# An edge mask written by VectorE into the scores' bank in place of a mask product on TensorE

## The chip, the cores and the metric

The kernel runs on one core of a Trainium2 chip. The metric is the device time of one launch in microseconds (us). Before the change it is 702.63 us, the median of three runs (699.69 to 703.38).

A core has a matrix engine (TensorE, PE in the profile; its weight loads have a row of their own, PEld), VectorE (DVE), ScalarE (ACT), GpSimd (POOL) and SyncE (SP), which issues the DMAs. Each takes its instructions in the order of the program, and semaphores between them hold an instruction until its inputs are there.

## The reference

One transformer block with modulation by a condition vector (2048 rows, width 448, 16 heads of 28, feed-forward width 1792). The part that the change touches is attention within a window:

```
scores = einsum("bhqd,bhkd->bhqk", q, k) * (Dh ** -0.5)
mask = (idx[:, None] - idx[None, :] >= 0) & (idx[:, None] - idx[None, :] < W)     # W = 256
scores = where(mask, scores, -1e9)
p = softmax(scores, axis=-1)
o = einsum("bhqk,bhkd->bhqd", p, v)
```

A query attends to itself and to the 255 rows before it. Around it stand a layer norm with scale and shift, the products with wqkv and wo, a second layer norm and a feed-forward network with Mish.

## The kernel before

All large products run as several passes over values split into a high and a low half. The 2048 rows are worked on in four groups of 512 (g = 0 to 3). The qkv products of a group are written to DRAM with keys and queries transposed, and loaded per head.

Attention walks over 64 slots (16 heads of each of 4 groups; a slot is called a head below), and each head over three units b = 0, 1, 2, so that u = 3 x head + b. A unit is one bank of 512 columns of scores, keys along the partitions and queries along the columns. BLOCKS says which 128-row key blocks against which 128-row query tiles share the bank: the outer units hold a block three tiles wide and one a single tile wide, the middle unit two blocks two tiles wide. In group 0 the blocks before the first row are missing, so the middle unit holds one block, in columns 256 to 511.

B(u), line 733, makes a unit. It takes one of two banks (tag sB, in turn), multiplies keys and queries into it (L742; the first product overwrites the bank, the next ones add), and then adds the mask: an identity matrix (identr) is the stationary operand and a strip of fdmask the moving one, so that the product puts 0 or -2^100 onto the scores. fdmask has two triangles, one for the far edge of the window (key too old) and one for the diagonal (key too new), 128 columns each. In groups 1 to 3 the outer units get by with one product over two separate strips of 128 columns (L753), since some rows of the operands carry a part of their mask; the middle unit has its far triangle in columns 128 to 255 and its diagonal in 256 to 383, and one product of 256 columns covers both (L757). In group 0 the middle unit has the diagonal alone, one product of 128 columns on the same line, and the outer units have theirs there too. ScalarE then takes the exponential of the bank twice, to P in f32 and to Ph, the high half (L760 and L761).

The order on the engines is written out by hand. In the step of unit u the program issues, in this order: what is due of earlier small work (pipe.step: splits of the qkv products, layer norm outputs); the products of the low parts with the values for unit u - 3 (PV, L778) and, at a head's end, the copy-out of its sums (EV, L784); B(u); the subtraction P - Ph for unit u - 1 on GpSimd (SP, L768); the first scores of a head three ahead (A, L711, in one of two banks with tag sA), whose row maxima VectorE takes under a mask (L713, tile mx); at some heads the transposition of these maxima (M2, L719); a share of the filler work (the qkv products of the next group, the products with wo of the group before, L315, and transpositions, L250), by a credit of so much per unit; a piece of side work (layer norms, L241 and L220, weight sums, L175); and the products of the high parts for unit u - 2.

VectorE's queue in this stretch therefore holds, in the order of issue: low halves of the fillers (L339, L369, L262, L647), the reductions (L713), the small splits of the maxima (L721, L722), the sums for the outputs (L805, L806) and the side work.

The mask fdmask is made once at the start: fdf is a piece of a weight buffer (wmf) that is free by then; GpSimd clears it (L463) and cuts the two triangles (L464, L466), and ScalarE copies it twice, side by side, into the 512 columns of fdmask in bf16 (L513).

Of the kernel before, what the change touches and what calls it, by code (L numbers as in the profile page):

```python
# [11 lines left out]
AF = mybir.ActivationFunctionType  # L12
ALU = mybir.AluOpType
# [38 lines left out]
def adaln_block(ctx: ExitStack, tc: tile.TileContext, x, wqkv, wo, w1, b1, w2, c, w_mod, out):  # L52
    nc = tc.nc
    PE, ACT, DVE, POOL = nc.tensor, nc.scalar, nc.vector, nc.gpsimd
# [37 lines left out]
    def bank(tag, bufs, name):  # L92
        return PS[0].tile([128, 512], F32, name=name, tag=tag, bufs=bufs)
# [18 lines left out]
    for k in range(4):  # L112
        wmf = st0.tile([128, 2 * D], F32, name=f"wm01_{k}")
# [11 lines left out]
    two = wqkv[:, 128:1152].rearrange("r (a n) -> r a n", n=512)[:, :, 0:256]  # L125
# [30 lines left out]
    identr = kq.tile([128, 128], BF16, name="identr")  # L156
    fdmask = kq.tile([128, 512], BF16, name="fdmask")
# [301 lines left out]
    for v in V:  # L459
        POOL.memset(v[:, :, 28:29].bitcast(F32), 1.0)  # L460
        POOL.memset(v[:, :, 29:32].bitcast(F32), 0.0)
    fdf = wmf[:, 0:256]
    POOL.memset(fdf[:, 0:256], 0.0)  # L463
    POOL.affine_select(fdf[:, 128:256], fdf[:, 128:256], pattern=[[-1, 128]], compare_op=ALU.is_ge, fill=-2.0 ** 100,  # L464
                       base=-1, channel_multiplier=1)
    POOL.affine_select(fdf[:, 0:128], fdf[:, 0:128], pattern=[[1, 128]], compare_op=ALU.is_ge,  # L466
                       fill=-2.0 ** 100, base=0, channel_multiplier=-1)


# [40 lines left out]
    flush()  # L510
    split_cols(*QCOLS[2], (POOL, POOL, DVE, DVE))
    for c in (0, 256):
        ACT.activation(fdmask[:, c:c + 256], fdf, AF.Copy)  # L513
    st0_s.close()
    att, att_s = pool("att")
    Q2 += [att.tile([128, 2, GT], F32R, name=f"q2_{i}") for i in range(1, NQ // 2)]
# [26 lines left out]
    def two(v, c, step):  # L543
        return bass.AP(v.tensor, v.offset + c, [list(v.ap[0]), [step, 2], [1, 128]])
# [182 lines left out]
    def units(g, b):  # L727
        return [x for x in BLOCKS[b] if g > 0 or x[0] >= 2]

    def by_width(blocks):  # L730
        return sorted(blocks, key=lambda x: x[2] - x[1])

    def B(u):
        i, b = divmod(u, 3)
        g, h = divmod(i, H)
        q, k = Q3[i % NQ], K3[i % NK]
        bl = units(g, b)
        c0 = bl[0][3]
        rows = 86 if g == 0 else 128
        p = bank("sB", 2, f"sB{u}")  # L740
        for n, (jj, t0, t1, c) in enumerate(by_width(bl)[::-1]):
            PE.matmul(p[:, c:c + 128 * (t1 - t0)], k[0:rows, jj * 128:(jj + 1) * 128], q[0:rows, t0 * 128:t1 * 128],  # L742
                      start=(n == 0), stop=False, skip_group_check=True)
        far = {c + 128 * (jj - t0) for jj, t0, t1, c in bl if t0 <= jj < t1}
        diag = {c + 128 * (jj - 2 - t0) for jj, t0, t1, c in bl if t0 <= jj - 2 < t1}
        masked = []
        for c in sorted(far | diag):
            if c in far:
                masked.append((256 if c + 128 in diag else 128, c, 128))
            elif c - 128 not in far:  # L750
                masked.append((128, c, 0))
        if g and b != 1:
            PE.matmul(two(p, (64, 0)[b // 2], 320), identr, two(fdmask, (192, 0)[b // 2], 192), start=False, stop=True,  # L753
                      skip_group_check=True)
            masked = []
        for n, c, m in sorted(masked):
            PE.matmul(p[:, c:c + n], identr, fdmask[:, m:m + n], start=False, stop=True, skip_group_check=True)  # L757
        P = Pt[u] = att.tile([128, 512], F32, name=f"P{u}", tag="P", bufs=3)
        Ph[u] = att.tile([128, 512], F32R, name=f"Ph{u}", tag="Ph", bufs=3)
        ACT.activation(P[:, c0:], p[:, c0:], AF.Exp, scale=SCALE)  # L760
        ACT.activation(Ph[u][:, c0:], p[:, c0:], AF.Exp, scale=SCALE)  # L761
# [7 lines left out]

    def PV(u, P):  # L770
        i, b = divmod(u, 3)
        g, h = divmod(i, H)
        if P is Ph and b == 0:
            pvb[i] = bank("sA", 2, f"pv{i}") if NS - 3 <= i < NS - 1 else bank("pv", 1, f"pv{i}")
        pv = pvb[i]
        for n, (jj, t0, t1, c) in enumerate(by_width(units(g, b))):
            j = 4 * g - 2 + jj
            PE.matmul(pv[0:60, t0 * 128:t1 * 128], V[j % NV][:, h, :], P[u][:, c:c + 128 * (t1 - t0)],  # L778
                      start=(P is Ph and b == 0 and n == 0), stop=False, skip_group_check=True)

# [287 lines left out]
    for u in range(NU + 9):  # L1068
        s, k = divmod(u, 3)
        g = s // H  # L1070
# [8 lines left out]
        if u < NU:  # L1079
            B(u)  # L1080
# [28 lines left out]
        if to_copy and u % 6 == 5:  # L1109
            t, p = to_copy.pop(0)  # L1110
# [20 lines left out]
    p1 = FW["p1"]  # L1131
# [65 lines left out]
    for n in range(NN + 1):  # L1197
        g, f = divmod(n, NF)
# [47 lines left out]
```

## Time and profile before

| what | value |
|---|---|
| timed runs | 699.69, 702.63, 703.38 us |
| profiled execution, its own time | 699.71 us |
| its span in the trace | 698.0 us |
| attention stretch | about 48 to 403 us |
| score products of B (L742) | 352, 73.7 us busy |
| mask products (L753 and L757) | 96 and 128 |
| row-maximum reductions (L713) | 256, mean 527 ns |
| exponentials (L760 and L761) | 192 each, means 571 and 568 ns |
| low parts on GpSimd (L768) | 192, mean 1232 ns |

A row of a group gives line, engine, operation, output and inputs by the program's names, shapes, count, then busy time and the mean duration of one, and last the idle time of the engine before them with what ended it. A row of the timeline gives start, duration, engine, line, operation and, in brackets, an idle time ahead and its releaser. Durations of products on TensorE are whole flights through a pipelined array: products follow each other at shorter distances than these.

### The profile page before, as it was taken

Reading aid. Unit: us, or ns where it says so; the run is one execution under the profiler, and the core shown is the slowest. Engines: PE = TensorE matmul, PEld = TensorE weight load, DVE = VectorE, ACT = ScalarE, POOL = GpSimd, SP = SyncE. Lnnn points to the kernel's source line nnn. Section 1 sums busy time; section 2 is a strip of 40 time slices with the busy share of each in tenths; the row PEclk is TensorE's granted clock in tenths of the full one; section 3 lists DMA queues with packets and bytes.
Section 4 is the critical chain, followed back from the end, with each engine's and each line's share of the span. In section 5 each row is a group of like instructions: output and inputs, shape, how many; then the busy total and the mean of one; then the engine's idle time right before and its main releaser. Section 6 shows DMA issues by size and latency. Waiting matters only on the chain.

```text
span 698.0 us, 11835 instructions
## 1 busy us (share of the span) xinstructions
PE 679.1 (97%) x3905; PEld 583.6 (84%) x3905; DVE 382.2 (55%) x1030; ACT 391.7 (56%) x741; POOL 334.0 (48%) x372
## 2 busy tenths in 40 slices
PE   8899999999999999999999899999999999999997
PEld 8777788888888888888887688888888888888886
DVE  5688657688665887655768754553125212521112
ACT  4638788777667867667878874353224222422221
POOL 7846779686766776666779967222010000000000
PEclk9999999999999999999999999999999999999999
DMA  7865665365662462763773165810250035001001
GB/s 213 263 226 198 217 213 176 119 201 164 179 206 85 156 211 89 191 211 108 226 217 112 53 211 173 212 29 4 103 120 1 2 105 121 0 2 53 0 1 53
DMA packets 75568, 91.13 MB, mean 131 GB/s; under 512 B 31632, under 2 KB 51838, under 8 KB 75508
## 3 DMA queue, kind: packets, MB, share of 16 engines
q1 hardware_dynamic: 75044, 90.38, 42.5%
q8 instruction: 31, 0.51, 0.3%
q14 instruction: 29, 0.24, 0.1%
q10 hardware_dynamic: 464, 0.00, 0.0%
HBM read 56.60 MB, written 32.51 MB: 128 GB/s over the span
## 4 chain that ended last, share of the span: by engine, by line
PE 82%; DVE 6%; DMA 4%; issue 2%; ACT 2%; POOL 1%; SPq 1%; POOLq 0%; DVEq 0%; ACTq 0%
PE z L950 21%; PE pv L778 9%; PE qk L315 7%; PE acc L1142 7%; PE acc L1140 6%; PE acc L1141 6%; PE sA L711 5%; PE wo L315 5%; PE sB L742 4%; PE qk_v L315 4%; DMA scr<-st 2%; DVE junk L713 2%; PE et L792 2%; PE warm L428 1%; PE sB L753 1%
## 5 line engine op out<-in xcount | busy, mean ns | idle before, releaser
L768 POOL TENSOR_TENSOR Pl<-P,Ph 128x512 fp32r<-128x512 f32 (+2 forms) x192 | 235.0, 1232 | 77.5 <-ACT Ph L761 44.9
L713 DVE CUSTOM_DVE_ANT_0 junk<-sA,mask 128x384 f32<-128x384 f32 (+2 forms) x256 | 135.0, 527 | 91.9 <-PE sA L711 84.5
L760 ACT ACTIVATE P<-sB 128x512 f32<-128x512 f32 (+2 forms) x192 | 109.6, 571 | 58.8 <-PE sB L757 33.7
L958 DVE TENSOR_TENSOR al<-t,ah 128x512 fp32r<-128x512 f32 x56 | 39.2, 699 | 188.6 <-ACT ah L957 188.6
L956 ACT ACTIVATE t<-z,b1c 128x512 f32<-128x512 f32 x56 | 38.4, 686 | 142.9 <-PE z L950 142.6
L761 ACT ACTIVATE Ph<-sB 128x512 fp32r<-128x512 f32 (+2 forms) x192 | 109.0, 568 | 0.0
L711 PE MATMUL sA<-k,q 84*128 84x384 f32 (+2 forms) x256 | 100.7, 396 | 2.6 <-DVE mx L713 1.8
L950 PE MATMUL z<-hlf,w 128*128 128x512 f32 x224 | 88.5, 395 | 0.0
L950 PE MATMUL z<-hhf,w 128*128 128x512 f32 x224 | 88.5, 395 | 0.0
L1140 PE MATMUL acc<-w2h,ah 128*128 128x448 f32 x224 | 82.0, 366 | 0.0
L1142 PE MATMUL acc<-w2h,al 128*128 128x448 f32 x224 | 81.9, 366 | 0.0
L1141 PE MATMUL acc<-w2l,ah 128*128 128x448 f32 x224 | 81.5, 364 | 0.0
L778 PE MATMUL pv<-Ph,v 128*60 128x256 f32 (+2 forms) x352 | 76.7, 292 | 0.6 <-ACT o L784 0.3
L778 PE MATMUL pv<-Pl,v 128*60 128x256 f32 (+2 forms) x352 | 73.8, 283 | 2.9 <-POOL Pl L768 2.0
L742 PE MATMUL sB<-q,k 128*128 128x256 f32 (+1 forms) x352 | 73.7, 283 | 0.6 <-DMA q<-mr 0.6
L950 PE MATMUL z<-hhf,w1l 128*128 128x512 f32 x168 | 66.3, 394 | 0.0
L742 PEld LDWEIGHTS sB<-q,k 128*128 128x128 f32 (+1 forms) x352 | 61.2, 188 | 2.0 <-DMA q<-mr 1.0
L778 PEld LDWEIGHTS pv<-Ph,v 128*60 128x60 f32 x352 | 45.7, 133 | 14.1 <-ACT o L784 1.9
L711 PEld LDWEIGHTS sA<-k,q 84*128 84x128 f32 x256 | 49.6, 195 | 8.0 <-DVE mx L713 5.3
L778 PEld LDWEIGHTS pv<-Pl,v 128*60 128x60 f32 x352 | 45.1, 132 | 11.9 <-POOL Pl L768 4.0
L950 PEld LDWEIGHTS z<-hlf,w 128*128 128x128 f32 x224 | 42.1, 188 | 10.1
L224 POOL COPY xn<-xn 128x64 f32<-128x64 f32 x12 | 4.5, 396 | 93.7 <-DVE xn L241 93.6
(167 smaller groups left out, 1305.0 us busy)
## 6 DMA issues: line engine op xcount, KB each, us to landing
scr<-st SPq DMA_DIRECT2D x24, 512.0 KB
k<-scr SPq DMA_DIRECT2D x48, 252.0 KB
q<-scr SPq DMA_DIRECT2D x64, 168.0 KB
scr<-st SPq DMA_DIRECT2D x32, 256.0 KB
x<-x1d SPq DMA_DIRECT2D x10, 448.0 KB
xin<-in_A_x_dram SPq DMA_DIRECT2D x8, 448.0 KB
xr<-in_A_x_dram SPq DMA_DIRECT2D x16, 224.0 KB
x1d<-xr SPq DMA_DIRECT2D x16, 224.0 KB
```

The lines of the kernel that those rows point to most:

```text
L315: PE.matmul(p, b, a, start=(n == 0), stop=(n == 10))
L711: PE.matmul(p[:, c0:384], q[0:84, t * 128:(t + 1) * 128], k[0:84, t * 128 + c0:t * 128 + 384], start=True, stop=True)
L713: DVE.tensor_tensor_reduce(out=junk[:, c0:384], in0=p[:, c0:384], in1=mask[:, c0:384], scale=1.0, scalar=-3.0e38, op0=ALU.add, op1=ALU.max ...
L742: PE.matmul(p[:, c:c + 128 * (t1 - t0)], k[0:rows, jj * 128:(jj + 1) * 128], q[0:rows, t0 * 128:t1 * 128], start=(n == 0), stop=False, ski ...
L760: ACT.activation(P[:, c0:], p[:, c0:], AF.Exp, scale=SCALE)
L761: ACT.activation(Ph[u][:, c0:], p[:, c0:], AF.Exp, scale=SCALE)
L768: eng.tensor_tensor(Pl[u][:, a:b], Pt[u][:, a:b], Ph[u][:, a:b].bitcast(F32), op=ALU.subtract)
L778: PE.matmul(pv[0:60, t0 * 128:t1 * 128], V[j % NV][:, h, :], P[u][:, c:c + 128 * (t1 - t0)], start=(P is Ph and b == 0 and n == 0), stop=F ...
L950: PE.matmul(zb[n], ps[m][1], ps[m][0], start=(m == 0), stop=(m == 10))
L1140: PE.matmul(p, ah[n][:, ts], w2h[f], start=(f == 0), stop=False)
L1141: PE.matmul(p, ah[n][:, ts], w2l[f], start=False, stop=False)
L1142: PE.matmul(p, al[n][:, ts], w2h[f], start=False, stop=(f == NF - 1))
```

## The change

In the step of a head's first unit (b = 0, except for the very first head), behind that unit's products, the bank of the next unit, the middle one, is taken at once, and VectorE copies the mask into it, over all its columns: 512 in groups 1 to 3, 256 in group 0. When the middle unit's turn comes, its first product no longer overwrites the bank but adds to it, and its mask product is left out. For this the mask is laid out as the middle unit needs it: 128 columns of zero, the far triangle, the diagonal, 128 columns of zero. The outer units' products keep their form and read their strips at other places of it. The middle unit of the first head keeps its mask product.

```diff
-    fdf = wmf[:, 0:256]
-    POOL.memset(fdf[:, 0:256], 0.0)
+    fdf = wmf[:, 0:512]
+    POOL.memset(fdf, 0.0)
     POOL.affine_select(fdf[:, 128:256], fdf[:, 128:256], pattern=[[-1, 128]], compare_op=ALU.is_ge, fill=-2.0 ** 100,
                        base=-1, channel_multiplier=1)
-    POOL.affine_select(fdf[:, 0:128], fdf[:, 0:128], pattern=[[1, 128]], compare_op=ALU.is_ge,
+    POOL.affine_select(fdf[:, 256:384], fdf[:, 256:384], pattern=[[1, 128]], compare_op=ALU.is_ge,
                        fill=-2.0 ** 100, base=0, channel_multiplier=-1)
...
     for c in (0, 256):
-        ACT.activation(fdmask[:, c:c + 256], fdf, AF.Copy)
+        ACT.activation(fdmask[:, c:c + 256], fdf[:, c:c + 256], AF.Copy)
...
+    seeds = {}
+
     def B(u):
...
-        p = bank("sB", 2, f"sB{u}")
+        seeded = u in seeds
+        p = seeds.pop(u) if seeded else bank("sB", 2, f"sB{u}")
         for n, (jj, t0, t1, c) in enumerate(by_width(bl)[::-1]):
             PE.matmul(p[:, c:c + 128 * (t1 - t0)], k[0:rows, jj * 128:(jj + 1) * 128], q[0:rows, t0 * 128:t1 * 128],
-                      start=(n == 0), stop=False, skip_group_check=True)
+                      start=(n == 0 and not seeded), stop=False, skip_group_check=True)
...
-                masked.append((128, c, 0))
-        if g and b != 1:
-            PE.matmul(two(p, (64, 0)[b // 2], 320), identr, two(fdmask, (192, 0)[b // 2], 192), start=False, stop=True,
-                      skip_group_check=True)
+                masked.append((128, c, 256))
+        if g and b != 1 and not seeded:
+            c, d, m, n = ((64, 320, 192, -64), (320, -320, 192, 64))[b // 2]
+            PE.matmul(two(p, c, d), identr, two(fdmask, m, n), start=False, stop=True, skip_group_check=True)
             masked = []
-        for n, c, m in sorted(masked):
+        for n, c, m in sorted(masked) if not seeded else ():
             PE.matmul(p[:, c:c + n], identr, fdmask[:, m:m + n], start=False, stop=True, skip_group_check=True)
+        if u and b == 0:
+            p1 = seeds[u + 1] = bank("sB", 2, f"sB{u + 1}")
+            d = units(g, b + 1)[0][3]
+            DVE.tensor_copy(p1[:, d:], fdmask[:, d:])
```

## The prediction

> **What bounds the kernel now.** I read the page's head and its chain of work first, then the busy time of the attention stretch, where every edit of the change lies.
>
> ```profile
> PE 679.1 (97%) x3905; PEld 583.6 (84%) x3905; DVE 382.2 (55%) x1030; ACT 391.7 (56%) x741; POOL 334.0 (48%) x372
> ...
> PE 82%; DVE 6%; DMA 4%; issue 2%; ACT 2%; POOL 1%; SPq 1%; POOLq 0%; DVEq 0%; ACTq 0%
> ```
>
> TensorE (PE) is busy 97% of the span and holds 82% of the chain that ended last; VectorE (DVE) holds only 6% of it. A product that is taken away from PE should therefore shorten the kernel by nearly its own time, as long as nothing else makes PE stand still. But the mean hides the stage: VectorE's work is crowded into the attention stretch, from 48 to 403 us.
>
> ```profile
> 48.00:403.00 355.00, 344.10 (x2308) 294.22 (x2307) 255.62 (x787) 271.28 (x549) 261.71 (x246) 1.00 0.54 167
> ```
>
> The columns after the length are PE, weight loads (PEld), DVE, ACT and POOL. PE is at 97% with a granted clock of 1.00, and DVE is at 255.62 of 355, that is 72%. So the change takes work from the engine at 97% and gives work to one at 72%, in a stretch where PE already waits for DVE at a few places:
>
> ```profile
> PEld sA L711 <- DVE mx L713: 5.3, 13, 0.8
> ...
> PEld pv L778 <- POOL Pl L768: 4.0, 7, 0.8
> ...
> PEld mt L719 <- DVE mx L713: 2.4, 3, 0.9
> ...
> PEld pv L778 <- ACT o L784: 1.9, 5, 0.6
> ```
>
> The columns are microseconds in total, times, and the longest. PE's waits on the row-maximum reductions (mx) come to 5.3 + 2.4 = 7.7 us; those on POOL and ACT, which this change doesn't touch, to 5.9 us.
>
> **What is removed.** The middle unit of each head (b = 1) loses its mask product and the load of the identity for it, except in head 0. The first row below holds this form's 64 wide products: 48 of them are middle units of groups 1 to 3; the other 16 lie in the last units of group 0 and stay. Of the 64 narrow ones 15 go.
>
> ```profile
> L757 PE MATMUL sB<-fdmask,identr 128*128 128x256 bf16 x64 | 18.0, 281 | 0.0
> L757 PE MATMUL sB<-fdmask,identr 128*128 128x128 bf16 x64 | 12.0, 228 | 0.0
> ```
>
> The 281 ns are a pipelined product's whole flight, not its price. The price is what it adds to the distance between its neighbours' starts, which the timeline shows:
>
> ```profile
> 247.64 0.28 PE L757 MATMUL sB<-fdmask,identr 128*128 128x256 bf16 x1
> ...
> 247.64 0.20 PEld L711 LDWEIGHTS sA<-k,q 84*128 84x128 f32 x1
> 247.68 0.42 PE L711 MATMUL sA<-k,q 84*128 84x384 f32 x1
> ...
> 247.94 0.37 PE L315 MATMUL wo<-wo,hlo 128*128 128x448 f32 x1
> ...
> 248.56 0.34 PE L711 MATMUL sA<-k,q 84*128 84x384 f32 x1
> ...
> 248.73 0.40 PE L778 MATMUL pv<-Ph,v 128*60 128x128 f32 x2
> ```
>
> From the mask product to the product behind the sA product there are 247.94 - 247.64 = 0.30 us; an sA product without a mask ahead takes 248.73 - 248.56 = 0.17 to its follower. The rows have two digits, so 0.13 is good to 0.02; I take 0.12. For the narrow form, of half the columns, I take 0.07, an estimate between a half of that and the whole. The sum: 48 x 0.12 + 15 x 0.07 = 5.8 + 1.0 = 6.8 us off PE, all in the stretch where PE is at 97%. The bounds are 48 x 0.11 + 15 x 0.06 = 6.2 and 48 x 0.13 + 15 x 0.12 = 8.0.
>
> **What is added.** 63 writes of VectorE from bf16 in SBUF to f32 in PSUM: 512 columns in 48 heads, 256 in 15. The trace has no such form. The nearest rows:
>
> ```profile
> L254 DVE TENSOR_SCALAR tr<-tr,cols 128x512 f32<-128x512 f32 x14 | 11.4, 812 | 0.7 <-ACT hh L257 0.7
> ...
> L713 DVE CUSTOM_DVE_ANT_0 junk<-sA,mask 128x256 f32<-128x256 f32 x16 | 6.7, 417 | 3.0 <-PE sA L711 2.7
> ...
> L254 DVE TENSOR_SCALAR zt<-zt,cols 128x512 f32<-128x512 f32 x12 | 6.3, 523 | 0.0
> ...
> L786 DVE COPY o<-pv 60x512 f32<-60x512 f32 x3 | 2.1, 684 | 0.1
> ```
>
> The plain copy of 512 columns with one side in PSUM took 684 ns. The same tensor_scalar (L254) took 523 ns with both sides in SBUF and 812 with both in PSUM; these two are my ends. I take 0.68 and, from the 256-column row, 0.42: 48 x 0.68 + 15 x 0.42 = 32.6 + 6.3 = 38.9 us more on DVE, which takes it from 72% to (255.6 + 38.9) / 355 = 83% of the stretch.
>
> [...]
>
> Most of these microseconds are hidden under PE. What counts is whether a write is done when PE comes to the middle unit's score products. The write goes to the bank that the last unit of the head before has used, so it starts when two things are over: ACT's second exponential of that unit (Ph, L761), and whatever stands ahead of it in DVE's in-order queue. It must be done before the first sB product (L742) of the middle unit. With 0.05 us after the release and 0.06 from its end to PE, I worked this through for all 63 heads on the trace's own times. Four of them, each as the release by ACT, where it matters the DVE instruction ahead, and the middle unit's first product:
>
> ```profile
> 55.14 0.59 ACT L761 ACTIVATE Ph<-sB 128x512 fp32r<-128x512 f32 x1
> ...
> 56.46 0.69 DVE L262 TENSOR_TENSOR hl<-tr,hh 128x512 fp32r<-128x512 f32 x1
> 56.48 0.28 PE L742 MATMUL sB<-q,k 86*128 86x256 f32 x1
> ```
>
> ```profile
> 250.51 0.59 ACT L761 ACTIVATE Ph<-sB 128x512 fp32r<-128x512 f32 x1
> ...
> 251.33 1.44 DVE L241 TENSOR_SCALAR xin<-xin,mva,rsa 128x448 f32<-128x448 f32 x1
> ...
> 252.96 0.40 PE L742 MATMUL sB<-q,k 128*128 128x256 f32 x2
> ```
>
> ```profile
> 330.64 0.59 ACT L761 ACTIVATE Ph<-sB 128x512 fp32r<-128x512 f32 x1
> ...
> 331.28 0.68 DVE L339 TENSOR_TENSOR st<-qk,st 128x512 fp32r<-128x512 f32 x1
> ...
> 332.86 0.40 PE L742 MATMUL sB<-q,k 128*128 128x256 f32 x2
> ```
>
> ```profile
> 394.63 0.59 ACT L761 ACTIVATE Ph<-sB 128x512 fp32r<-128x512 f32 x1
> ...
> 395.40 0.40 PE L742 MATMUL sB<-q,k 128*128 128x256 f32 x2
> ```
>
> The first is the first late one: DVE is free at 57.15, the write ends at 57.15 + 0.05 + 0.42 = 57.62, and PE wanted it at 56.48: 57.62 + 0.06 - 56.48 = 1.2 us late. The second: 252.77 + 0.05 + 0.68 + 0.06 - 252.96 = 0.6 late. The third is one of the hidden ones: 331.96 + 0.79 = 332.75, ahead of 332.86. The fourth is the last late one: ACT is done at 395.22, and 395.22 + 0.79 - 395.40 = 0.6 late. In all 17 of 63 are late, by 8.3 us together, 3.0 in group 0 and 5.3 behind it; the other 46 are hidden by the products between the head's first and middle unit, often with a microsecond to spare. With the writes at 0.52 and 0.32 the sum is 6.2 us, at 0.81 and 0.50 it is 10.5.
>
> Behind each write stand the reductions of the head three ahead (L713), then the transposed maxima and the low halves of the qkv products. They start up to 0.68 later, and PE waits for them before the next sA product and the transposition of the maxima, 7.7 us now. One in four reductions has a write right ahead; DVE's free time falls from 28% to 17% of the stretch. I take half of the present wait more, 3.5 us, an estimate; the bounds are 1 and 8.
>
> Against this, PE's waits on POOL and ACT (5.9 us) give way where PE comes later anyway: 2 us off, bounds 0 and 4. The sum: -6.8 + 8.3 + 3.5 - 2 = +3.0 us.
>
> The rest costs nothing. The prepared mask is 512 columns in place of 256, so one POOL memset doubles, by 0.31 us, and the instruction behind the masks waits 0.94 us for ACT today:
>
> ```profile
> 22.01 0.31 POOL L463 MEMSET wm<- 128x256 f32 x1
> ...
> 23.87 1.16 POOL L198 TENSOR_TENSOR wql<-wqs,wq 128x448 fp32r<-128x448 f32 x1 [0.94 <-ACT wq L192]
> ```
>
> If that cover were gone it would be 0.3 us once. The two remaining wide products read other columns of the mask in the same amount, and no DMA is moved.
>
> The profiled execution took 699.71 us, for a span of 698.0; the three timed runs were 699.69, 702.63 and 703.38, median 702.63, mean 701.9. On the profile's own time the sum gives 702.7. I carry it to the mean of the runs: 701.9 + 3.0 = 704.9.
>
> **Rivals.** *The write hides.* Once PE has waited for one late write, all its later work stands later against DVE, and the late writes were counted one by one on the old times; the neighbours with a microsecond to spare speak for it. That 5.3 of the 8.3 us come from the same kinds of DVE work ahead in each group (the low halves, the layer norm's scaling) speaks against it. With half of the late time, and 1 us in place of 3.5 behind: -6.8 + 4.2 + 1 - 2 = -3.6, so 698.3.
>
> *POOL holds the write.* The scaling of L241 (SBUF to SBUF) takes 0.50 us alone and up to 1.46 beside POOL's low parts:
>
> ```profile
> L241 DVE TENSOR_SCALAR xin<-xin,mva,rsa x12: 499/611/1455, 41.1 to 251.3; 128x448 f32<-128x448 f32 x12
> ```
>
> ```profile
> L241 DVE TENSOR_SCALAR xin<-xin,mva,rsa 128x448 f32<-128x448 f32 x12 | 10.1, 842 | 0.5 <-POOL rsa L235 0.5
> ```
>
> Its mean is 842, 0.34 above the free value. If the write, which also reads SBUF, were held in this way, it would take 0.34 more: the late sum becomes 15.0 us, the waits behind it 5, and the kernel -6.8 + 15.0 + 5 - 2 = +11.2, so 713. It becomes the slower side as soon as a write takes over 0.75 on average. The reductions of L713 also read from SBUF (their mask) with the other operand in PSUM, and show no such tail, which speaks against it:
>
> ```profile
> L713 DVE CUSTOM_DVE_ANT_0 junk<-sA,mask x256: 258/557/559, 34.4 to 390.2; 128x384 f32<-128x384 f32 x112, 128x128 f32<-128x128 f32 x16
> ```
>
> Their median of 557 ns is 2 ns under their longest. [...]
>
> *The saving isn't there.* If PE's weight loads set the pace (294 of 355 us busy), the sA load would move up only in part. With half the saving: +3.0 + 3.4 = +6.4, so 708.3. Against it speaks that the load before the sA product (0.20 us, L711 in the first timeline rows) overlaps the mask product, and that an sA product without a mask ahead goes on after 0.17.
>
> **How the numbers follow.** The forecast gets 0.55, the hidden write 0.22, POOL's hold 0.10, the missing saving 0.13. A measurement of this kernel can tell about 0.5% from no change, 3.5 us. The forecast's own range runs from 0 to +6.5, by the bounds of its terms (701.9 to 708.4), and gives 0.01 to faster, 0.36 to same and 0.18 to slower; the hidden write 0.14 to faster and 0.08 to same; the other two 0.02 to faster or same and 0.21 to slower. So 0.15 faster, 0.46 same, 0.39 slower. The range, 698 to 711.5, takes in the hidden write and the missing saving and leaves out most of POOL's hold.
>
> **What would show it.** In the profile after: 63 new DVE rows of a copy or cast into sB, at 0.68 and 0.42 (0.52 or over 0.75 would be a rival's); 65 products in place of 128 on the line of L757; a wait of PE on that copy of some 8 us in 15 to 20 places, the largest in group 0 beside the low halves (L262); PE's wait on mx up from 7.7 to about 11 us. A wait of PE on the copy below 4 us would make the forecast wrong on the fast side; a mean write of 1 us on the slow side. A gain of over 3.5 us would mean that the late sum doesn't stand, whatever the length of the write.

## The result and the profile after

The change takes 707.33 us, the median of six runs (705.29 to 709.80), beside 701.13 us for the kernel before, six runs in turn with it (699.69 to 703.38). The ratio is 1.0099, with an interval of 1.0082 to 1.0116: 6.9 us slower, between 5.7 and 8.1. The forecast was 3.0 us slower, 704.9 us, with 0 to +6.5 us as its own range. These differences go by the ratio, here and below, so they can be some tenths off those of the medians. The profiled execution took 707.92 us, for a span of 706.3.

The head of the page, and its chain of work:

```profile
PE 676.7 (96%) x3842; PEld 580.2 (82%) x3842; DVE 416.2 (59%) x1093; ACT 392.3 (56%) x741; POOL 333.0 (47%) x372
...
PE 78%; DVE 9%; DMA 8%; issue 2%; SPq 1%; ACT 1%; POOL 0%; DVEq 0%; POOLq 0%; ACTq 0%
```

TensorE has 63 products less (3842 in place of 3905) and 2.4 us less to do, and yet the span is 8.3 us longer: its own share of the chain falls from 82% to 78%, VectorE's rises from 6% to 9% and the DMA's from 4% to 8%. The attention stretch, first with the bounds of before and then to its later end:

```profile
48.00:403.00 355.00, 335.67 (x2208) 286.49 (x2209) 283.80 (x840) 265.58 (x536) 254.73 (x239) 1.00 0.54 166
```

```profile
48.00:411.00 363.00, 341.94 (x2249) 291.13 (x2250) 290.39 (x852) 272.16 (x549) 260.48 (x246) 1.00 0.53 164
```

VectorE is now busy for 80% of the stretch, 72% before, and TensorE for 94 to 95% instead of 97%. The groups by form show the new writes (L764) and what is left of the mask products on the old L757, which now is L760:

```profile
L764 DVE CAST sB<-fdmask 128x512 f32<-128x512 bf16 x48 | 33.0, 687 | 4.6 <-ACT Ph L768 4.5
...
L760 PE MATMUL sB<-fdmask,identr 128*128 128x128 bf16 x49 | 8.6, 229 | 0.0
...
L764 DVE CAST sB<-fdmask 128x256 f32<-128x256 bf16 x15 | 6.4, 425 | 3.3 <-ACT Ph L768 3.3
...
L760 PE MATMUL sB<-fdmask,identr 128*128 128x256 bf16 x16 | 4.4, 275 | 0.0
```

The 63 writes took 0.687 and 0.425 us on average, 39.4 us in all, and 65 products are left. The waits over the whole span, in microseconds in total, times, and the longest:

```profile
PE sB L745 <- DVE sB L764: 5.3, 9, 1.4
PEld sA L711 <- DVE mx L713: 5.2, 11, 1.1
PEld mt L719 <- DVE mx L713: 4.0, 5, 0.9
PEld pv L785 <- POOL Pl L775: 3.7, 9, 0.7
...
PE sB L745 <- DMA q<-mr: 2.3, 2, 1.9
PEld pv L785 <- ACT o L791: 2.1, 5, 0.6
...
PEld sB L745 <- DVE sB L764: 1.1, 2, 0.6
```

TensorE waits for the write, as forecast; it waits for the maxima 9.2 us (7.7 before). Its waits on POOL and ACT are 5.8 us (5.9 before). The four heads of the prediction's working, now in the timeline of after, with the work ahead of the write, the write, and the product that wants it:

```profile
57.44 0.69 DVE L262 TENSOR_TENSOR hl<-tr,hh 128x512 fp32r<-128x512 f32 x1
58.05 0.42 DVE L764 CAST sB<-fdmask 128x256 f32<-128x256 bf16 x1
...
58.61 0.35 PE L745 MATMUL sB<-q,k 86*128 86x256 f32 x1 [0.98 <-DVE sB L764]
...
257.26 1.30 DVE L241 TENSOR_SCALAR xin<-xin,mva,rsa 128x448 f32<-128x448 f32 x1
...
258.48 0.68 DVE L764 CAST sB<-fdmask 128x512 f32<-128x512 bf16 x1
...
259.31 0.47 PE L745 MATMUL sB<-q,k 128*128 128x256 f32 x2 [0.36 <-DVE sB L764]
...
337.20 0.68 DVE L339 TENSOR_TENSOR st<-qk,st 128x512 fp32r<-128x512 f32 x1
...
337.80 0.68 DVE L764 CAST sB<-fdmask 128x512 f32<-128x512 bf16 x1
...
338.63 0.48 PE L745 MATMUL sB<-q,k 128*128 128x256 f32 x2
...
402.45 0.59 ACT L768 ACTIVATE Ph<-sB 128x512 fp32r<-128x512 f32 x1
402.51 0.69 DVE L262 TENSOR_TENSOR hlf<-trf,hhf 128x512 fp32r<-128x512 f32 x1
403.12 0.68 DVE L764 CAST sB<-fdmask 128x512 f32<-128x512 bf16 x1
...
403.86 0.50 PE L745 MATMUL sB<-q,k 128*128 128x256 f32 x2 [0.36 <-DVE sB L764]
```

Three of them are late as worked out. The third (head 50) was forecast 0.11 us early and is 0.11 late. Its product starts 0.15 us after the end of the write (338.48 to 338.63), not 0.06, and VectorE itself has come nearer to TensorE here: from the end of L339 to the product there were 0.89 us before (331.96 to 332.86) and are 0.75 now (337.88 to 338.63). In the fourth (head 62) the write begins at the end of a low half (L262), not of the exponential that the prediction took as its release.

The lists of waits leave out a part of what a late product costs, so I took the balance from the products themselves. Every kernel here issues the same 3681 products besides the mask products, in the same order. For each of them I compared its start with that of before, and took by how much this shift differs from the shift of the product ahead. Summed over the attention, from the first product of unit 0 to that of the last unit, this gives how much longer the attention takes in the profile. An sA product counts as later from some 0.02 us on. The columns are the change, its second profile (the last run below), and seven of the experiments:

| us against before | change | again | e1 | e2 | e4 | e9 | e5 | e7 | e8 |
|---|---|---|---|---|---|---|---|---|---|
| first product of the middle unit, 18 heads | 8.56 | 8.59 | 0.02 | 8.31 | 0.02 | 3.40 | 1.87 | 20.77 | 0.02 |
| sA products that come later | 3.07 | 4.30 | 0.91 | 1.88 | 2.00 | 5.01 | 1.75 | 9.46 | 0.00 |
| transposed maxima (mt) | 1.45 | 1.42 | 0.01 | 1.39 | 1.19 | 0.67 | -0.63 | 1.43 | 0.01 |
| first product of head 8 (waits for a DMA) | 1.33 | 2.05 | 0.34 | 1.75 | 0.25 | 2.36 | 0.43 | -0.31 | 0.54 |
| other score products of B | 1.67 | 1.41 | 0.17 | 1.22 | 0.88 | 2.07 | 1.37 | 5.92 | -0.02 |
| products with the values (pv) | -0.62 | -0.27 | 0.14 | -0.28 | 0.72 | 1.07 | 1.33 | -1.09 | -0.06 |
| sA products that come sooner, and all others | -8.26 | -8.39 | -7.53 | -1.56 | -6.22 | -4.11 | -8.41 | -4.59 | -0.95 |
| sum | 7.20 | 9.12 | -5.94 | 12.71 | -1.16 | 10.48 | -2.29 | 31.59 | -0.46 |

The 18 heads of the first row are those whose product waited for the write in the change: 2, 3, 4, 21, 22, 24, 37, 38, 40, 50, 52, 53 and 58 to 63. The column of e8, the kernel before itself, shows what two profiles of one kernel differ by: half a microsecond at head 8, and 0.95 in the row of the forward shifts, 0.8 of it at a single sA product behind unit 47.

### The profile page after: what moved, and what is told of

It reads as the page before. It is cut to its first block, busy times and chain, and to the rows that moved or that the text cites. A ratio compares the mean times of both kernels' runs of the same rounds, so it can differ in the third digit from the quotient of the medians.

```text
span 706.3 us, 11771 instructions
## 1 busy us (share of the span) xinstructions
PE 676.7 (96%) x3842; PEld 580.2 (82%) x3842; DVE 416.2 (59%) x1093; ACT 392.3 (56%) x741; POOL 333.0 (47%) x372
## 4 chain that ended last, share of the span: by engine, by line
PE 78%; DVE 9%; DMA 8%; issue 2%; SPq 1%; ACT 1%; POOL 0%; DVEq 0%; POOLq 0%; ACTq 0%
PE z L957 20%; PE pv L785 8%; PE qk L315 7%; PE acc L1149 6%; PE acc L1147 6%; PE acc L1148 6%; PE sA L711 4%; PE sB L745 4%; PE qk_v L315 4%; PE wo L315 4%; DMA scr<-st 3%; DVE junk L713 3%; DMA xr<-in_A_x_dram 2%; PE warm L428 1%; SPq L59 1%
## 5 line engine op out<-in xcount | busy, mean ns | idle before, releaser
L711 PE MATMUL sA<-k,q 84*128 84x384 f32 (+2 forms) x256 | 95.5, 377 | 3.7 <-DVE mx L713 2.6
L745 PE MATMUL sB<-q,k 128*128 128x256 f32 (+1 forms) x352 | 75.6, 289 | 8.3 <-DVE sB L764 5.3
L791 ACT ACTIVATE o<-pv 60x512 f32<-60x512 f32 x61 | 36.0, 590 | 23.7 <-PE pv L785 23.3
```

Of the source, the lines that this page charges most:

```text
L711: PE.matmul(p[:, c0:384], q[0:84, t * 128:(t + 1) * 128], k[0:84, t * 128 + c0:t * 128 + 384], start=True, stop=True)
```

## The experiments

Theory A is the prediction's: each mask product is worth about a tenth of a microsecond, and the writes cost what the late ones hold up, directly and by what stands behind them on VectorE. The rivals change from run to run and are in the expectations.

**The saving alone (e1).**

```diff
-        seeded = u in seeds
+        seeded = u > 1 and b == 1
...
-                      start=(n == 0 and not seeded), stop=False, skip_group_check=True)
+                      start=(n == 0), stop=False, skip_group_check=True)
...
-            DVE.tensor_copy(p1[:, d:], fdmask[:, d:])
```

> The middle units from head 1 on have neither write nor mask product; their scores stay unmasked, and their exponentials take a 64th of the scale so that they stay finite. Theory A (late writes): the removed products are worth their distance between starts, 48 x 0.12 + 15 x 0.07 = 6.8 us, so 701.1 - 6.8 = 694.3, ratio 0.990. Theory B (the saving is mostly not there, because weight loads or other waits take its place): 698 to 701, ratio 0.995 to 1.000. Theory C (group 0's long wait for the maxima's DMA and the clock's dip behind it make the difference, not the writes): as A.

It took 695.06 us against 700.52: a ratio of 0.9926 (0.9908 to 0.9945), 5.2 us faster. In the balance 7.5 us of forward shifts come out where 6.8 were forecast (e8 has 0.95 in this row without any edit), and 1.6 of them are given back: 0.9 at sA products, 0.3 at head 8, 0.3 elsewhere. TensorE comes sooner and meets VectorE where VectorE was before. The saving is there.

**The write alone (e2).** The write is made, and then the product overwrites it and the mask product follows as before.

```diff
-        seeded = u in seeds
-        p = seeds.pop(u) if seeded else bank("sB", 2, f"sB{u}")
+        seeded = False
+        p = seeds.pop(u) if u in seeds else bank("sB", 2, f"sB{u}")
```

> The write stands as in the change, but the middle unit's first product overwrites the bank and its mask product is kept, so that nothing is saved on TensorE. Theory A: the late writes measured in the changed kernel (8.6 us) and 3 to 5 us of waits for reductions behind them, 701.1 + 12 = 713, ratio 1.017. Theory B: only what the changed kernel lost, 701.1 + 6 to 7 = 708, ratio 1.009. Theory C: 704 to 706, of which most in group 0.

It took 711.75 us against 700.52, a ratio of 1.0159 (1.0136 to 1.0183): 11.1 us slower. The two halves add up: -5.2 + 11.1 = +5.9, and the change itself is +6.9 (5.7 to 8.1). The late products are the same, 8.31 us, so it matters little whether the saving is there: which heads are late is set in the main by VectorE's queue, not by how soon TensorE comes.

**The writes of groups 1 to 3 (e3).** Group 0 keeps its mask products.

```diff
-        if u and b == 0:
+        if g and b == 0:
```

> The write and the saving in groups 1 to 3 only; group 0 as before, with its 15 narrow mask products. Theory A: group 0 has 2.8 of the 8.6 us of late writes and 1.0 of the 6.8 us saved, so it is worth about 2 us: 707.3 - 2 = 705.3, ratio 1.006. Theory C: group 0 holds nearly all, 702, ratio 1.001 or less.

It took 705.46 us against 700.52, a ratio of 1.0072 (1.0055 to 1.0089), as forecast. Group 0 costs 2 us of the change's 6.9; its three late writes alone are 1.15 + 0.09 + 1.61 = 2.85 us.

**The writes that nobody waits for (e4).** The 18 late heads keep the mask product; 45 heads have the write.

```diff
-        if u and b == 0:
+        if u and b == 0 and i not in (2, 3, 4, 21, 22, 24, 37, 38, 40, 50, 52, 53, 58, 59, 60, 61, 62, 63):
```

> The write in only those 45 heads in which the changed kernel's trace has it done before TensorE comes to the middle unit; the 18 others keep their mask product. Theory A: no late writes, 33 x 0.12 + 12 x 0.07 = 4.8 us saved, 1 to 3 us of it lost to reductions that start later: 697.3 to 699.3, ratio 0.996. Theory B: 701 to 703, ratio 1.000 to 1.003. Theory C: 701 or more, since the writes of group 0 are mostly kept.

It took 700.06 us against 700.52, a ratio of 1.0006 (0.9987 to 1.0025). Here theory A missed. No product waits for a write any more, and 33 wide and 12 narrow mask products are gone, but nothing is gained. The waits of this kernel say where it went:

```profile
PEld sA L711 <- DVE mx L713: 5.3, 13, 0.7
...
PEld mt L719 <- DVE mx L713: 3.8, 5, 0.9
```

The wait before the transposition of the maxima is 3.8 us where it was 2.4, with no late write in the kernel. In the balance 6.2 us of forward shifts stand against 2.0 at sA, 1.2 at the maxima, 0.9 at other score products and 0.7 at the products with the values. By groups, group 0 keeps its saving (-1.24 us, -1.44 in e1), and groups 1 to 3 gain nothing from 33 wide products (+0.08, -4.5 in e1). A hidden write still holds the reduction behind it.

**The write on ScalarE (e5).**

```diff
-            DVE.tensor_copy(p1[:, d:], fdmask[:, d:])
+            ACT.activation(p1[:, d:], fdmask[:, d:], AF.Copy)
```

> The change, but ScalarE writes the mask in place of VectorE, at the same place of the program. ScalarE itself frees the bank (its second exponential), so the write follows at once and VectorE's queue is as before the change. Theory A (the loss comes from VectorE's queue): the saving stays (5.2 us as measured alone), few writes are late, 1 to 3 us lost because ScalarE's exponentials come 0.6 us later: 701 - 5 + 2 = 698, ratio 0.994 to 0.999. Rival B (any engine that writes late on the way from one unit's exponential to the next but one's products costs the same): 705 to 708, ratio 1.006 to 1.010.

It took 698.35 us against 700.14, a ratio of 0.9967 (0.9952 to 0.9982): faster than both kernels, by 2.3 us and some 9. The groups by form:

```profile
L764 ACT ACTIVATE sB<-fdmask 128x512 f32<-128x512 bf16 x48 | 29.0, 604 | 0.9
...
L764 ACT ACTIVATE sB<-fdmask 128x256 f32<-128x256 bf16 x15 | 5.8, 389 | 0.3
```

ScalarE writes the same bank in 604 ns, hardly waits before it, and has just read the bank itself, so its write stands right behind that reading in its own queue. The first products of the middle unit in those 18 heads come to 1.87 us. With the same mask in the same bank at the same place of the program, only the engine differs, so the loss comes from the write's place in VectorE's queue, and rival B is out. Single runs reach e1's time: three of the twelve took 695.0 to 695.8 us.

**The write ahead of the low halves (e6, and e9 with the banks as they were).** In e6 the write is issued at the start of the head's first step, before that step's low halves.

```diff
+    def seed(u):
+        seeds[u] = bank("sB", 2, f"sB{u}")
+        p1 = seeds[u + 1] = bank("sB", 2, f"sB{u + 1}")
+        d = units(u // 3 // H, 1)[0][3]
+        DVE.tensor_copy(p1[:, d:], fdmask[:, d:])
...
+        if 0 < u < NU and k == 0:
+            seed(u)
         pipe.step()
```

> The change with the write issued ahead of the small work that is due in the head's first step, so that low halves no longer stand ahead of it on VectorE. Theory A: of the 8.6 us of late writes some 5 us go (those with L262 or L647 ahead), 1 to 3 us come back because these low halves are later: 707.3 - 5 + 2 = 704, ratio 1.003 to 1.007. Rival B (it is the extra load on VectorE, whatever its place): as the change, 706 to 708, ratio 1.008 to 1.011.

It took 714.04 us against 700.14, a ratio of 1.0209 (1.0186 to 1.0232), worse than the change, and outside both theories. The waits of this kernel show why it tests neither:

```profile
PEld sB L745 <- ACT Ph L764: 18.9, 35, 1.4
PE sB L745 <- ACT Ph L764: 8.6, 25, 1.2
...
PE sB L745 <- DVE sB L770: 1.2, 4, 0.4
```

TensorE waits for the write 1.2 us now, but 8.6 us for the exponentials (L764 in this kernel). Banks are handed out in the order of first use; the write came first and took the bank that was free, and the head's first unit got the one that ScalarE was still reading. In its trace all 63 first units start behind the exponentials of the unit just before (29 of 63 in the change), and 30 writes begin ahead of the end of those. (So the middle units always sat in the same bank. I take it that head 16's, the first there with its left half, then lacks a part of its mask; no run shows that by itself.) e9 does the same with two fixed banks, each unit in the one that it has in the change:

```diff
+    SB = [bank(f"sB{n}", 1, f"sB{n}") for n in range(2)]
...
+        p = SB[u % 2]
...
+        seeds.add(u + 1)
+        p1 = SB[(u + 1) % 2]
```

> This kernel makes the write at the head's first step ahead of the low halves and evictions of that step, as e6 did, but with two fixed scores' banks, so that the units keep the banks they have in the change. In e6 the write came first in the program and so was given the bank that came free first, which the head's first unit then lacked: product waits for the exponentials' reading of the unit just before (8.6 us of PE waits in 25 places that the change does not have). Everything is computed. Theory A (VectorE's load is the cost: whoever comes first, somebody behind it is late): the waits of PE for the write nearly go (e6: 1.2 us in 4 places where the change has 5.3 in 9), the low halves, evictions and reductions get later by as much, and the time stays near the change's: 1.007, between 1.004 and 1.010. e6's ratio without its 8.6 us of bank waits gives the same: 714.0 - 8.6 = 705.4, 1.0075. Theory B (only the late copy costs, what it displaces has room): the change's gain of 0.9926 less a little: 0.996 to 1.001. If it comes near 1.02 again, the bank was not what made e6 dear.

It took 707.63 us against 700.38, a ratio of 1.0097 (1.0065 to 1.0129), the change's own. Its waits:

```profile
PEld sA L711 <- DVE mx L713: 7.1, 14, 1.1
...
PE sB L746 <- DVE sB L771: 2.1, 6, 0.6
```

The late products fall from 8.6 to 3.4 us, and the time is no better. The balance has to be read by groups here, because this profile has two windows of 6.83 us at half the granted clock (0.50 from 57.3 to 64.1 us, in group 0, for the one; 0.990 on the mean), which can cost 3.4 us each. Group 0 loses 7.4 us (3.2 in the change, 3.9 in its second profile). Groups 1 to 3 lose 3.0 us (4.0 and 5.3): their late products fall from 5.7 to 3.1 us, and of these 2.6 us the sA products give back 0.5, those with the values 0.3 and the forward shifts 0.9, since the low halves are later. That is 4.0 - 2.6 + 1.7 = 3.1, so the second window does not show there.

Theory B is out: even the fastest of the six runs took 703.67 us, at a clock of 0.999. Theory A's ratio came, but the runs of this kernel reach from there to 710.21 us at a clock of 0.990, so a part of its time is half speed and not late work. In groups 1 to 3 most of what an earlier write wins is paid by those behind it, and 1 to 2 us are left.

**Each write made twice (e7).**

```diff
             DVE.tensor_copy(p1[:, d:], fdmask[:, d:])
+            DVE.tensor_copy(p1[:, d:], fdmask[:, d:])
```

> The change with every write made twice over the same bank, 1.37 and 0.85 us in all. Theory A: the sum over late writes, worked out as in the prediction on the times of the kernel before, grows from 8.3 to 22.1 us in 27 places, so 707.3 + 13.8 and 1 to 3 us more behind it: 721 to 724, ratio 1.030 to 1.033. Rival B (the cost goes with VectorE's load): the 39 us that the writes added cost 11.1 us, so another 39 us cost as much again, 718, ratio 1.025. Rival C (the loss is in the disturbances of group 0): 710 or less.

It took 733.17 us against 700.14, a ratio of 1.0477 (1.0458 to 1.0496). Another 39 us of writes cost 26 us where the first cost 11. The late products grow from 8.6 to 20.8 us and the sA products' loss from 3.1 to 9.5: the second writes of the 18 late heads take some 11.7 us, and the products behind them come 12.2 us later, so there the second write is paid in full. Theory A (721 to 724) and rival B (718) were both too low. In the profile five windows of 3.4 us at half the granted clock lie in the attention as well (0.50 from 70.3 to 73.7 us for one; 0.988 on the mean), some 1.7 us each at most, 8.5 in all. With all of that taken off, 724.7 us are left, near theory A's 724, so how much of the miss is late work stays open.

**The kernel before once more (e8).** No edit.

> The kernel before, for a second trace of it: how much its start, its wait for the maxima's DMA at head 8 and its granted clock differ from one execution to the next. Theory A with the disturbances as chance: the shifts against the first trace are 0 to 1 us at the start and 0 to 2 us at head 8, as in the changed kernels. If they belong to the change: both are 0, and the clock is 1.00 without a dip.

It took 699.77 us; its products come 0.55 us later than the first profile's at the attention's start and 0.1 at its end. Its wait at head 8 was 1.1 us, the first profile's 0.6, and its clock 1.00. So the start and head 8 do differ by chance, here by half a microsecond.

**ScalarE's write in a part of the groups (e10 and e11).**

```diff
-        if u and b == 0:
+        if 0 < u < 3 * H * 3 and b == 0:
```

> ScalarE writes the mask in groups 0 to 2; in group 3 the mask product stays. Everything is computed. In the profile of the kernel with ScalarE's write in all groups the attention's groups stood at -1.4, -1.3, -1.7 and +2.0 us against the kernel before, and the two half-speed windows of TensorE's clock (3.4 us each, so 1.7 us lost in each) both fell into group 3. Theory A (group 3 is where ScalarE's write costs, and the half-speed windows follow from the waits there): 0.9937, a gain of 4.4 us, and no half-speed window inside the attention. Theory B (the loss in group 3 was chance, the remainder of 2.9 us between that kernel and the one without write or mask is spread over all heads): 48 of 63 heads of the gain of 2.3 us, 0.9975.

```diff
-        if u and b == 0:
+        if g and b == 0:
```

> ScalarE writes the mask in groups 1 to 3; in group 0, where the mask product is 128 columns wide and PE waits on a transfer at head 8 for 0.6 to 2.9 us from profile to profile, the mask product stays. Everything is computed. Theory A (ScalarE's write hides, and each of the 48 wide products that it replaces gives back 0.10 us): group shifts of about 0, -1.3, -1.6 and -1.2 us, -4.1 us in all, 0.9942, between 0.992 and 0.996. Theory B (what the kernel with ScalarE's write in all groups lacks against the one without write or mask, 2.9 us, is a cost of ScalarE's write in every head, which the profiles did not happen to show): 48 of 63 of its gain, 0.9975.

e10 (groups 0 to 2) took 699.43 us against 700.38, a ratio of 0.9989 (0.9969 to 1.0009); e11 (groups 1 to 3) 697.88 against 699.86, 0.9973 (0.9957 to 0.9990). Theory A missed twice, and theory B's number lies in both intervals: neither group 3 nor group 0 is the one place where ScalarE's write costs. In the profiles group 1 saves 1.6 us in both, as in e1, and group 2 saves 1.6 and 1.0; group 3 saves nothing in e11, although no window at half the granted clock lies in it (1.000 on the mean), and 1.2 in e1. In group 0, where e5 and e10 run the same code, the one saves 1.4 us and the other loses 0.2, so single profiles differ by as much as what is left to explain. What else takes the remaining part of e1's 5.2 us stays open.

**The change once more (e12).** No edit.

> The change once more, unaltered, beside the kernel before on this chip. If the transfer that PE waits on at head 8 and the half-speed window of TensorE's clock behind it are chance, this profile shows another wait there (0.6 to 2.9 us in the profiles so far) and perhaps no window; the waits for the write come again in the same heads, 8 to 9 us late in all, and the ratio again lies between 1.008 and 1.012. If the change causes the window, it stands at the same place behind the head-8 wait.

It took 708.17 us against 699.86, a ratio of 1.0118 (1.0097 to 1.0139). The late products fall on the same 18 heads with the same lengths, to 0.03 us each: 8.59 in all. The wait at head 8 is 2.6 us, and a half-speed window stands at the same place behind it, which by the expectation speaks for the change as its cause. Against this stands that e3 and e11, whose group 0 has no write, waited 2.1 and 2.2 us there, and e7, with each write made twice, 0.3. The window isn't what makes the change slow: two of its runs with a mean clock of 1.000 took 706.47 and 707.25 us. The windows of the change, then those of this run: columns as above, the last three the granted clock, the DMA share and GB/s.

```profile
85.19:88.60 3.41, 1.49 (x10) 0.87 (x9) 0.94 (x5) 0.43 (x2) 1.35 (x1) 1.00 0.96 312
88.60:92.01 3.41, 3.41 (x17) 2.92 (x15) 1.89 (x7) 1.75 (x6) 2.25 (x3) 0.50 0.74 224
```

```profile
84.60:88.00 3.40, 0.76 (x6) 0.51 (x6) 0.33 (x1) 0.00 (x0) 1.11 (x1) 1.00 0.79 270
88.00:91.40 3.40, 3.40 (x14) 2.69 (x14) 2.06 (x8) 1.78 (x5) 1.64 (x3) 0.50 0.79 240
```

## Why the prediction was right in kind and too low by four microseconds

**The saving** was forecast at 6.8 us. e1 shows 7.5 us of forward shifts, inside the bounds of 6.2 to 8.0, and 5.2 by its time. The rival *the saving isn't there* (half of it) is out, though its 708.3 us lie nearer to the measured 707.33 than the forecast's 704.9 do: the time alone would have chosen the wrong one. What the prediction did not see is that a saving, too, is partly given back: TensorE arrives sooner at reductions that are no sooner, 0.9 us in e1 without any write.

**The length of the write** was right: 0.687 and 0.425 us against 0.68 and 0.42. The rival *POOL holds the write* is out: the longest of 63 took 0.695 us, although GpSimd was busy beside 58 of them for more than half of their length.

**The late writes** were right: 8.3 us in 17 heads were forecast, 8.56 in 18 came, 2.85 in group 0 (forecast 3.0) and 5.71 behind it (5.3). The rival *the write hides* is out: the delays did not thin out. (That the units ahead are late by about the same amount on all engines is a likely reason, not shown.) The lists of waits show only 5.3 + 1.1 us of it in 11 places; the rest is booked on other releasers or on none, as at head 50.

That the sums agree so closely is in part luck. Worked through again on the trace's exact times, the prediction's rule gives 9.2 us in 18 heads: in head 62 the low half L262 ends at 395.37, behind the exponential, so that the write is 0.76 late and not 0.6, and head 63 is late too, by 0.57. Of these 18, heads 19 and 35 (0.32 each) were not late in the change, and 50 and 59 were. And two of the rule's margins were wrong in opposite ways: a write starts 0.08 us before the row of the instruction ahead of it ends (258.48 against 258.56 above), not 0.05 behind it, and most products start 0.15 us behind the write, not 0.06.

**The waits behind the writes** were forecast at 3.5 us more. In the balance the sA products and the maxima lose 4.5 us, within the bounds of 1 to 8, and 0.9 of that e1 loses without a write; in the lists the wait for the maxima grew from 7.7 to 9.2 us instead of about 11. e4 shows this term alone: it is what eats the gain of the 45 hidden writes. It was right in kind, and between right and 1.0 too low in size.

**"PE's waits on POOL and ACT (5.9 us) give way where PE comes later anyway: 2 us off"** did not come as told: by the lists these waits are still 5.8 us. In the balance the products with the values and the forward shifts together get back 0.76 + 0.73 = 1.5 us at most beyond e1's, so in size the term is only about half a microsecond off. GpSimd and ScalarE take their work from TensorE, so they may simply come later with it; that reason is argued, not shown.

**What was not in the sum** is 3.0 us, the largest part of what the forecast was short of: head 8's first product loses 1.33 and the other score products 1.67 us. Head 8 waits for the DMA of its row maxima, 0.6 us in the first profile of before and 1.1 in the second, 1.9 and 2.6 in the two of the change, but also 2.1 and 2.2 in e3 and e11, which have no write so early; so a part is chance, and how much is the change's stays open. The half-speed window behind it costs about another 1.3 us (units 25 and 26 lose 0.98 and 0.29 us to before) and is booked in part under the score products, in part under the others. The sum by the change's own profile: -7.53 + 8.56 + 4.52 - 1.35 + 3.00 = 7.20, where -1.35 is what the last two rows but the sum gain on -7.53 (-0.62 and -0.73). The forecast was -6.8 + 8.3 + 3.5 - 2 = +3.0. Up to 2.6 us of the 7.20 are head 8 and the window, and runs without the window lack its part; since two such runs of the change are 5.3 and 7.4 us slower than the kernel before beside them, this balance explains its own profile and not every run.

**The range** of 0 to +6.5 us was not what the bounds of the terms add up to: that is -4.8 to +12.3. The measured +6.9 us (5.7 to 8.1) lie just beyond the upper end of the narrow one, with an interval that reaches into it.

## What to carry to other kernels

Moving work off a full engine is worth what the receiving engine can take at the moments when it is wanted: here VectorE was busy for 72% of the stretch, and 39 us of writes cost 11, three quarters of it in 18 of 63 places, 16 of which could be worked out from the trace of before. A write that nobody waits for is not free either; ask who stands behind it in its queue, and give it, as in e5, to the engine that frees the buffer itself. Count a saving on the critical engine only up to the next thing it will wait for, and look after a re-ordering experiment whether the buffers still rotate as before.

## What the runs showed of the hardware

TensorE's granted clock was halved for a single window of 3.41 us behind a stretch of the same length in which it had been busy only 1.49 us (0.76 in the second profile of the change), at a wait of 1.9 and 2.6 us. In the window 17 products ran where 21 did before, and two products of 512 columns started 0.42 us apart (89.35 and 89.77 us), 0.23 in the kernel before (89.47 and 89.70). The clock was also 0.50 in e9 from 57.3 to 64.1 us and in e7 from 70.3 to 73.7 us; its mean over the profile was 0.998 and 0.996 in the two of the change, 0.997 in e2, 0.995 in e5 (two windows in group 3), 0.993 in e6, 0.988 in e7 and 0.990 in e9. In e3, e10 and e11 waits of 2.1, 1.9 and 2.2 us at head 8 brought none: the mean was 1.000.

A short busy time alone did not bring it either. In e3 TensorE was busy for 1.30 us of the 3.40 from 83.00 us, in the change for 1.86 of the 3.41 from 64.71, and the clock was 1.00 in both stretches and behind them. What else it takes is not shown.
